# Gated linear attention and a soft mixture of experts on one core: the DRAM rows of q, k, f, v and the weights cut to 512 bytes

## The chip, the core and the metric

The kernel runs on one core of a Trainium2 chip. The metric is device time in microseconds (us), the median over runs of the same program; lower is better. A profile is one execution, recorded instruction by instruction and DMA packet by DMA packet. The engines are PE (matrix multiplies, with PEld for their weight loads), DVE, ACT and POOL (elementwise work) and SP, which here only issues DMAs; SPq is its queue in the profile. Sixteen DMA engines move what SP issues.

## The reference

Two parts follow each other. The first is a recurrence over 768 positions for 4 batches of 8 heads, each with a 48x48 state. The second takes its output as 3072 tokens of 384 numbers, mixes all tokens into 32 slots, runs a two-layer network of 8 experts over the slots, and mixes the slots back into tokens.

```python
f = 1.0 / (1.0 + np.exp(-f_logit))
for t in range(S):                                   # S = 768, D = 48
    state = f[:, :, t, :, None] * state + np.einsum('bhd,bhe->bhde', k[:, :, t], v[:, :, t])
    y[:, :, t] = np.einsum('bhd,bhde->bhe', q[:, :, t], state)
...
logits = x @ phi                                     # x: y as [3072, 384]; phi: [384, 32]
d = softmax over tokens;  slot_input = d.T @ x       # [32, 384]
h = np.maximum(slot_input[e] @ w1[e], 0.0)           # 8 experts, w1[e]: [384, 1024]
slot_out[e] = h @ w2[e]                              # w2[e]: [1024, 384]
out = softmax over slots @ slot_out                  # [3072, 384]
```

All data is float32. The time is taken without the host's rearrangement of the inputs (`_layout`), which only decides in what order numbers lie in DRAM.

## The kernel before

**Blocks.** The recurrence is cut into 24 blocks (NN = 24): 4 batches of 6 blocks of 128 positions, each block for all 8 heads at once. A block needs four inputs: f (the gate's logits), k, q (each 128 partitions x 512 numbers, 256 KB) and v (128 x 384, 192 KB). ACT turns f into logarithms of gates (lines 472 and 475), DVE scans them (464, 465), ACT takes exponentials of the scan (478, 479), POOL or DVE multiplies k and q by those (502, 505), PE transposes k (510), forms scores (524), the update of the state (536) and the outputs (555, 564, 574). Groups of four blocks then feed the softmax over tokens (623 to 657).

**Loads and buffers.** f is loaded one block at a time for the first two blocks and by pairs of blocks after that, into three buffers of two blocks each; k, q and v have four buffers each, used in turn. Tiles have short names: af and ag hold f, ak k, aq q, av v, ac the scans, as the scores, hm the "homes" that hold weights. In DRAM a block of k, q or f is one contiguous stretch of 256 KB with a row of 2 KB for every partition, and a block of v one of 192 KB with rows of 1536 bytes.

**Weights.** w1 and w2 are 12 pieces of 1 MB each. A piece is stored as [4, 128, 512]: four groups of 128 rows of 2 KB, and partition p gets row p of each group. The 12 pieces of w1 go into 12 homes while the recurrence runs (line 422), each held back until a given block has been planned. Three pieces of w2 go into three more homes, seven go into the buffers that the recurrence leaves free (af, ac, ag, ak, aq, as, av), and the last two into homes that w1 leaves free (line 426).

**What follows the recurrence.** PE multiplies the slots by w1 ("up", line 771), the result is transposed and masked, multiplied by w2 ("down", line 805), and the slots are mixed back into tokens (828) and stored in 12 DMAs of 384 KB (837).

**What sets the order.** Operations are added to a planner (`Plan.schedule`) with engines, dependencies, an estimated duration and a priority; it places each on an engine's queue, and the kernel then emits instructions in that order. Every engine works its queue in order. All loads and stores go through SP's single queue, so a load that waits for a buffer holds back all loads behind it, and SP's DMA number i also waits until its DMA number i - 8 has landed (the eight semaphores DMAHW0 to DMAHW7). For a load the planner uses its bytes, not its rows.

Of the kernel before, what the change touches and what calls it, by code (L numbers as in the profile page):

```python
# [15 lines left out]
B, H, S, D = 4, 8, 768, 48  # L16
BT = 128
HT = 64
NB = S // BT
NN = B * NB  # L20
DP = 64
PR = H // 2
# [9 lines left out]
CUT = (0, 128, 256, 384)  # L32
NPART = len(CUT) - 1
HOME = 2048
NHOME = 15
NX = 4

# [14 lines left out]
def flat(t):  # L52
    n = len(t.shape)
    if n == 2:
        return t
    names = "abcde"[: n - 1]
    return t.rearrange(f"p {' '.join(names)} -> p ({' '.join(names)})")
# [207 lines left out]
def gla_soft_moe_kernel(ctx: ExitStack, tc: tile.TileContext, q, k, f, v, fd, qd, kd, vd, phi, w1, w2, out):  # L265
# [9 lines left out]
    nc = tc.nc  # L275
# [18 lines left out]

    AF_, AC, AG, AK, AQ, AS, AV = (P([128, HOME], n) for n in ("af", "ac", "ag", "ak", "aq", "as", "av"))
    homes = [P([128, HOME], f"hm{i}") for i in range(NHOME)]
    NF, NK, NQ, NV, NSS, NXT = 3, 4, 4, 4, 3, 6
# [8 lines left out]
    fb = [group(AF_, 0), group(AF_, 1), group(AG, 0)]  # L306
    cb = [group(AC, i) for i in range(2)]
    kb = [part(AK, 512 * i, 512, a=PR) for i in range(NK)]
    qb = [part(AQ, 512 * i, 512, a=PR) for i in range(NQ)]
    vb = [part(AV, 384 * i, 384, a=H) for i in range(NV)]  # L310
# [103 lines left out]
    W1 = [(j, hf, c) for j in range(2) for hf in range(2) for c in range(3)]  # L414
    W2 = [(p, j, kh) for p in range(NPART) for j in range(2) for kh in range(2)]

    def runs(t):
        return t.rearrange("p (q n) -> p q n", q=4)

    def load_w1(x):  # L420
        t = w1p[W1[x]]
        return lambda e: nc.sync.dma_start(runs(t), w1[x].rearrange("q p n -> p q n"))

    def load_w2(p, j, kh):
        t = w2p[p, j, kh]
        return lambda e: nc.sync.dma_start(runs(t), w2[W2.index((p, j, kh))].rearrange("q p n -> p q n"))


    def T(n, stage):
        return 3.8 * n + stage  # L430

    def load(dst, src, name, key, prio, nbytes):
        add(name, {"SP": 0.42}, lambda e: nc.sync.dma_start(dst, src), w=key, prio=prio, bytes=nbytes)  # L433
# [3 lines left out]

    def load_f(n, cnt):
        i, o = n // 2 % NF, n % 2
        load(fb[i][:, o : o + cnt], f[n : n + cnt].rearrange("n p a t -> p n a t"), f"f{n}", [("f", i, x) for x in range(o, o + cnt)], T(n, -12), 262144 * cnt)  # L440

    def loads(n):
        load(kb[n % NK], k[n], f"k{n}", [("k", n % NK)], T(n, -9), 262144)
        load(qb[n % NQ], q[n], f"q{n}", [("q", n % NQ)], T(n, -8.5), 262144)
        load(vb[n % NV], v[n], f"v{n}", [("v", n % NV)], T(n, -7), 196608)

    def last_of(c_):

# [405 lines left out]
    for n in range(NN):  # L854
        cnt = 1 if n < 2 else 2 - n % 2 * 2
# [6 lines left out]
        x = len(plan.ops)  # L862
# [24 lines left out]
    ending = len(plan.ops)  # L887
    early = NHOME - len(W1)
    for x in range(early):
        w2p[W2[x]] = homes[len(W1) + x]  # L890
        add(f"w2{W2[x]}", {"SP": 0.42}, load_w2(*W2[x]), w=[("home", len(W1) + x), ("w2", W2[x])], prio=1.1e3 + x, bytes=128 * HOME * 4, after=[paced[22]])
    for x, key in enumerate(W1):
        add(f"w1{x}", {"SP": 0.42}, load_w1(x), w=[("home", x)], prio=1e3 + x, bytes=128 * HOME * 4, after=[paced[7 * x // 4]])
    t0, down, put_o, sums, put_s, combine, put_f, store = tail()
# [102 lines left out]
def _layout(inputs):  # L997
    import numpy as np

    a = {}  # L1000

    def rows(x, pad, later):

        x = x.reshape(B, 2, 2, 2, NB, BT, D).transpose(2, 0, 4, 3, 6, 1, 5)
        x = np.stack([x[0], later(x[1])], 4)
        x = np.concatenate([x, np.full((B, NB, 2, DP - D, 2, 2, BT), pad, np.float32)], 3)
        return x.reshape(NN, 128, PR, BT)

    a["q"] = rows(inputs["q"], 0, lambda x: x[..., ::-1])
    a["k"] = rows(inputs["k"], 0, lambda x: x[..., ::-1])  # L1010
    a["f"] = rows(inputs["f_logit"], 30, lambda x: x[..., ::-1, :])
    x = inputs["v"].reshape(B, PR, 2, NB, BT, D).transpose(1, 0, 3, 4, 2, 5)
    x = np.stack([x[p][:, :, ::-1] if p % 2 else x[p] for p in range(PR)], 3)
    a["v"] = x.reshape(NN, BT, H, D)
    for n, name in (("fd", "f_logit"), ("qd", "q"), ("kd", "k"), ("vd", "v")):
        a[n] = inputs[name].reshape(B * PR, 2, S, D).transpose(0, 1, 3, 2)

    heads = [2 * (2 * m + (o ^ r)) + r for r in range(2) for m in range(2) for o in range(2)]
    order = np.concatenate([np.arange(D * h, D * h + D) for h in heads])
    x = inputs["moe_phi"][order].reshape(PR, 2, D, NS)  # L1020
    x = np.concatenate([x, np.zeros((PR, 2, DP - D, NS), np.float32)], 2)
    a["phi"] = x.reshape(PR, 128, NS).transpose(1, 0, 2)
    x = inputs["moe_w1"][:, order].reshape(4, 2, 3, 128, 2, 512)
    a["w1"] = x.transpose(1, 4, 2, 0, 3, 5).reshape(12, 4, 128, 512)
    x = inputs["moe_w2"].reshape(4, 2, 2, 4, 128, NPART, 128)
    a["w2"] = x.transpose(5, 1, 2, 0, 4, 3, 6).reshape(12, 4, 128, 512)
    return {n: np.ascontiguousarray(x) for n, x in a.items()}


# [22 lines left out]
```

## Time and profile before

| what | value |
|---|---|
| median of 3 runs | 188.34 us (187.5 to 189.64) |
| the profiled execution's own time | 188.79 us |
| its span, first to last instruction | 187.1 us |
| granted TensorE clock, mean | 0.957 of full speed |
| PE, PEld, DVE, ACT, POOL busy | 78%, 59%, 63%, 53%, 26% of the span |
| DMA packets; bytes | 28234; 54.12 MB |
| DMA engines busy with SP's packets | 81.2% of 16 engines' span |

The profiled execution took 0.45 us more than the median, and 1.7 us more than its span; the latter is what lies outside the first and last instruction. Times inside the trace count from the span's start.

A DMA is carried out as packets. Each run of contiguous bytes of the DRAM side is one packet here: of SP's 28192 packets, 21504 are rows of 2 KB (128 for each of 24 blocks of q, k and f, and 512 for each of 24 weight pieces), 3072 are v's rows of 1536 bytes, 1536 are output rows of 3 KB, 128 are phi's rows of 512 bytes, and 1952 are the 4-byte semaphore updates with which each of the 16 DMA engines reports the end of its share of each of the 122 DMAs.

"DMA share" in a view by stretches of time is the sum of packets' times divided by 16 engines' time. It can exceed 1, because neighbouring packets of an engine overlap a little. "To landing" is the time from the start of a DMA's issue on SP to the last of its 16 semaphore updates.

The stages are: start-up, about the first 20 us; the recurrence, to about 141 us; "up", 142.2 to 152.7 us; "down", 155.6 to 166.3 us; mixing back and stores, to the end.

### The profile page before, as it was taken

The page shows a single profiled execution, that of the slowest core. Times are in us where ns is not written, and L with a number is a line of the kernel's source. Part 1 is how long each engine was busy: PE and PEld are TensorE (multiplying, and loading weights), DVE is VectorE, ACT ScalarE, POOL GpSimd, SP SyncE. Part 2 cuts the span into 40 slices and gives each one's busy share as a digit, 9 for nine tenths or more (in the row PEclk, how much of TensorE's full clock was granted, in tenths as well). Part 3 has the DMA queues.
Part 4 walks back from the last instruction along what each step waited for, and adds up shares of the span by engine and source line. Part 5 has one row for each costly group of instructions (what it writes and reads, how often), then busy time and mean ns, then how long its engine had stood idle before and what let it go on. Part 6 is the DMA issues. An engine that isn't in the chain of part 4 may idle for free.

```text
span 187.1 us, 7446 instructions
## 1 busy us (share of the span) xinstructions
PE 146.7 (78%) x3238; PEld 109.8 (59%) x3238; DVE 117.3 (63%) x223; ACT 99.1 (53%) x187; POOL 48.0 (26%) x56
## 2 busy tenths in 40 slices
PE   4976886999869978794975996969778999999500
PEld 4864765768758766574854684756533338974100
DVE  6679956999778888974959879474163114026400
ACT  5889855796865948684874464423531120016600
POOL 4142091334460271434056911520011000000000
PEclk9999999999987999999999699999999999999955
DMA  5999999799976999996896779996999248006990
GB/s 186 321 392 383 387 381 383 237 340 398 368 251 172 336 391 312 381 385 203 229 399 208 255 255 316 398 386 215 328 398 388 99 120 332 4 4 267 395 354 16
DMA packets 28234, 54.12 MB, mean 289 GB/s; under 512 B 1952, under 2 KB 5152, under 8 KB 28192
## 3 DMA queue, kind: packets, MB, share of 16 engines
q1 hardware_dynamic: 28192, 53.55, 81.2%
q8 instruction: 27, 0.44, 0.9%
q14 instruction: 15, 0.12, 0.2%
HBM read 48.82 MB, written 4.72 MB: 286 GB/s over the span
## 4 chain that ended last, share of the span: by engine, by line
PE 54%; issue 14%; DVE 10%; DMA 7%; ACT 4%; SPq 3%; POOL 1%; DVEq 0%; POOLq 0%; ACTq 0%
PE pr L524 7%; PE sg L805 6%; PE sg L771 6%; PE pr L574 6%; PE pr L555 5%; PE sg L510 4%; PE pr L564 4%; DMA ak<-in_k_dram 3%; DMA af<-in_f_dram 3%; PE sg L606 3%; PE pr L828 3%; PE sg L536 3%; PE sg L623 3%; SPq L433 3%; PE sg L651 3%
## 5 line engine op out<-in xcount | busy, mean ns | idle before, releaser
L502 POOL TENSOR_TENSOR ak<-ak,af 128x512 f32<-128x512 f32 x14 | 19.0, 1362 | 44.4 <-ACT af L478 35.5
L527 DVE TENSOR_TENSOR as<-pr,tri 128x768 f32<-128x768 f32 x24 | 22.7, 946 | 10.0 <-PE pr L524 9.9
L524 PE MATMUL pr<-aq,ak 48*64 48x64 f32 (+1 forms) x768 | 23.2, 252 | 5.5 <-issue 4.9
L524 PEld LDWEIGHTS pr<-aq,ak 48*64 48x64 f32 x768 | 20.0, 137 | 7.6 <-issue 6.2
L510 PE MATMUL sg<-ident,ak 128*128 128x128 f32 x96 | 15.8, 283 | 4.8 <-issue 2.8
L577 ACT COPY xT<-pr 128x512 f32<-128x512 f32 x22 | 12.7, 585 | 12.6 <-PE pr L574 12.6
L513 ACT COPY ag<-sg 128x512 f32<-128x512 f32 x19 | 11.1, 584 | 11.9 <-PE sg L510 11.8
L555 PE MATMUL pr<-aq,st 48*48 48x128 f32 x320 | 14.1, 278 | 3.5 <-issue 3.4
L505 POOL TENSOR_TENSOR aq<-aq,ac 128x512 f32<-128x512 f32 x11 | 15.0, 1369 | 6.5 <-DMA aq<-in_q_dram 4.7
L574 PE MATMUL pr<-as,av 128*48 128x64 f32 x384 | 15.6, 226 | 0.5 <-issue 0.5
L564 PE MATMUL pr<-as,av 64*48 64x64 f32 x384 | 11.6, 233 | 4.8 <-issue 2.4
L510 PEld LDWEIGHTS sg<-ident,ak 128*128 128x128 f32 x96 | 10.3, 140 | 8.2 <-issue 5.2
L606 PE MATMUL sg<-ident,xT 128*128 128x128 f32 x96 | 14.7, 280 | 0.0
L502 POOL TENSOR_TENSOR ak<-ak,ag 128x512 f32<-128x512 f32 x8 | 10.8, 1362 | 14.7 <-ACT ag L478 6.3
L574 PEld LDWEIGHTS pr<-as,av 128*48 128x48 f32 x384 | 12.5, 126 | 2.3 <-issue 1.7
L465 DVE TENSOR_TENSOR_SCAN ac<-chain,af 128x256 f32<-128x256 f32 x16 | 13.7, 858 | 0.0
L479 ACT ACTIVATE ac<-ac 128x1024 f32<-128x1024 f32 (+1 forms) x13 | 12.9, 994 | 0.3
L464 DVE TENSOR_TENSOR_SCAN ac<-chain,af 128x256 f32<-128x256 f32 x16 | 11.5, 717 | 2.4 <-ACT af L475 2.3
L564 PEld LDWEIGHTS pr<-as,av 64*48 64x48 f32 x384 | 8.5, 127 | 7.5 <-DVE as L527 3.9
L555 PEld LDWEIGHTS pr<-aq,st 48*48 48x48 f32 x320 | 8.6, 119 | 6.3 <-issue 5.6
L505 DVE TENSOR_TENSOR aq<-aq,ac 128x512 f32<-128x512 f32 x13 | 11.9, 937 | 0.1
L536 PE MATMUL sg<-av,ag 128*48 128x48 f32 x320 | 11.4, 215 | 0.5 <-ACT ag L513 0.5
(130 smaller groups left out, 256.1 us busy)
## 6 DMA issues: line engine op xcount, KB each, us to landing
hm<-in_w_dram SPq DMA_DIRECT2D x17, 1024.0 KB, 8.7
ak<-in_k_dram SPq DMA_DIRECT2D x24, 256.0 KB, 6.0
aq<-in_q_dram SPq DMA_DIRECT2D x24, 256.0 KB, 5.7
av<-in_v_dram SPq DMA_DIRECT2D x24, 192.0 KB, 5.9
out_dram<-hm SPq DMA_DIRECT2D x12, 384.0 KB, 4.1
af<-in_f_dram SPq DMA_DIRECT2D x7, 512.0 KB, 6.5
ag<-in_f_dram SPq DMA_DIRECT2D x4, 512.0 KB, 6.3
af<-in_w_dram SPq DMA_DIRECT2D x1, 1024.0 KB, 7.7
```

What stands on the lines that cost most here:

```text
L465: nc.vector.tensor_tensor_scan(cx[:, 2 * BT :][:, ::-1], chain, lx[:, 2 * BT :], 0.0, op0=ALU.mult, op1=ALU.add)
L479: add(f"p{n}", {"ACT": t_act(w)}, lambda e: nc.scalar.activation(flat(c_), flat(c_), AF.Exp, scale=-1.0), w=cs, prio=T(n, 1.2))
L502: tt(e)(flat(k_), flat(k_), flat(g_), op=ALU.mult)
L505: tt(e)(flat(q_), flat(q_), flat(c_), op=ALU.mult)
L510: nc.tensor.transpose(pk[:, a], k_[:, a], ident)
L524: nc.tensor.matmul(o, k_[rows[r], col(a), at], x, start=True, stop=True)
L527: tt(e)(sc_.rearrange("p r m t -> p (r m) t"), bank(("sc", n)).rearrange("p r (m t) -> p (r m) t", m=2)[:, :, :SW], tri.unsqueeze(1).broad ...
L536: nc.tensor.matmul(pk[rows[r], col(a)], kp_[:, col(a), rows[r]], v_[:, 2 * a + r], start=True, stop=True)
L555: nc.tensor.matmul(py[at : at + D, r, a // 2], s0[rows[r], col(a)], queries(r, a), start=a < 2, stop=False, skip_group_check=True)
L564: nc.tensor.matmul(py[at : at + D, r, a // 2, :HT], v_[by, 2 * a + r], sc_[by, r, a // 2, HT:BT], start=first and a < 2, stop=False, skip_ ...
L574: nc.tensor.matmul(py[at : at + D, r, a // 2, HT:], v_[:, 2 * a + r], sc_[:, r, a // 2, x : x + HT], start=False, stop=a >= 2, skip_group_ ...
L606: nc.tensor.transpose(px[:, i], xT[:, n % NXT, i], ident)
```

## The change

The arrays of q, k, f, v, w1 and w2 are laid out in DRAM in rows of 128 numbers, 512 bytes, where they had rows of 512 numbers (384 for v). A block of q, k or f becomes [4, 128, 128]: four groups of 128 rows, and partition p gets row p of each group. v becomes [3, 128, 128] and a weight piece [16, 128, 128]. Neighbouring rows of one partition then lie 64 KB apart. Each load still brings the same numbers to the same places of the same tile, where a partition's numbers lie side by side as before. phi and the stores are left as they are.

The load's access pattern names the rows on both sides, so that a 256 KB load has 512 rows in place of 128, a load of two blocks of f 1024 in place of 256, a load of v 384 in place of 128, and a weight piece 2048 in place of 512.

```diff
+RUN, VRUN = 128, 128
...
-    def runs(t):
-        return t.rearrange("p (q n) -> p q n", q=4)
+    def runs(t, n=RUN):
+        return t.rearrange("p (x n) -> p x n", n=n)

     def load_w1(x):
         t = w1p[W1[x]]
-        return lambda e: nc.sync.dma_start(runs(t), w1[x].rearrange("q p n -> p q n"))
+        return lambda e: nc.sync.dma_start(runs(t), w1[x].rearrange("x p n -> p x n"))

     def load_w2(p, j, kh):
         t = w2p[p, j, kh]
-        return lambda e: nc.sync.dma_start(runs(t), w2[W2.index((p, j, kh))].rearrange("q p n -> p q n"))
+        return lambda e: nc.sync.dma_start(runs(t), w2[W2.index((p, j, kh))].rearrange("x p n -> p x n"))
...
-        load(fb[i][:, o : o + cnt], f[n : n + cnt].rearrange("n p a t -> p n a t"), f"f{n}", [("f", i, x) for x in range(o, o + cnt)], T(n, -12), 262144 * cnt)
+        load(runs(flat(fb[i][:, o : o + cnt])), f[n : n + cnt].rearrange("n x p t -> p (n x) t"), f"f{n}", [("f", i, x) for x in range(o, o + cnt)], T(n, -12), 262144 * cnt)

     def loads(n):
-        load(kb[n % NK], k[n], f"k{n}", [("k", n % NK)], T(n, -9), 262144)
-        load(qb[n % NQ], q[n], f"q{n}", [("q", n % NQ)], T(n, -8.5), 262144)
-        load(vb[n % NV], v[n], f"v{n}", [("v", n % NV)], T(n, -7), 196608)
+        load(runs(flat(kb[n % NK])), k[n].rearrange("x p t -> p x t"), f"k{n}", [("k", n % NK)], T(n, -9), 262144)
+        load(runs(flat(qb[n % NQ])), q[n].rearrange("x p t -> p x t"), f"q{n}", [("q", n % NQ)], T(n, -8.5), 262144)
+        load(runs(flat(vb[n % NV]), VRUN), v[n].rearrange("x p t -> p x t"), f"v{n}", [("v", n % NV)], T(n, -7), 196608)
...
-        return x.reshape(NN, 128, PR, BT)
+        return x.reshape(NN, 128, PR * BT)
+
+    def runs(x, n=RUN):
+
+        return x.reshape(*x.shape[:2], -1, n).swapaxes(1, 2)
...
-    a["w1"] = x.transpose(1, 4, 2, 0, 3, 5).reshape(12, 4, 128, 512)
+    a["w1"] = x.transpose(1, 4, 2, 3, 0, 5).reshape(12, 128, HOME)
...
-    a["w2"] = x.transpose(5, 1, 2, 0, 4, 3, 6).reshape(12, 4, 128, 512)
+    a["w2"] = x.transpose(5, 1, 2, 4, 0, 3, 6).reshape(12, 128, HOME)
+    for n in ("q", "k", "f", "v", "w1", "w2"):
+        a[n] = runs(a[n], VRUN if n == "v" else RUN)
```

The planner sees the same bytes, dependencies and priorities, so on all five engines the instructions stand in the same order as before; only their line numbers and the loads' shapes differ. On SP's queue, around the point where the first weight pieces are loaded, before:

```order
L433 DMA af<-in_f_dram 128x2x512
L422 DMA hm_74<-in_w_dram 128x4x512
L433 DMA aq<-in_q_dram 128x512
L433 DMA ak<-in_k_dram 128x512
L422 DMA hm_75<-in_w_dram 128x4x512
L433 DMA av<-in_v_dram 128x384 x2
```

And in the changed kernel at the same place:

```order
L434 DMA af<-in_f_dram 128x8x128
L423 DMA hm_74<-in_w_dram 128x16x128
L434 DMA aq<-in_q_dram 128x4x128
L434 DMA ak<-in_k_dram 128x4x128
L423 DMA hm_75<-in_w_dram 128x16x128
L434 DMA av<-in_v_dram 128x3x128 x2
```

Nothing has moved: the last number of a shape, the length of a row, goes from 512 (or 384) to 128, and the number of rows for each partition grows to match.

More of the change, by code (lines that the diff above doesn't have):

```diff
@@ L1013, in _layout @@
     x = np.stack([x[p][:, :, ::-1] if p % 2 else x[p] for p in range(PR)], 3)
-    a["v"] = x.reshape(NN, BT, H, D)
+    a["v"] = x.reshape(NN, BT, H * D)
     for n, name in (("fd", "f_logit"), ("qd", "q"), ("kd", "k"), ("vd", "v")):
```

## The prediction

> **What bounds the kernel now.** The page's part on the DMAs comes first, since only loads change, with the waits for loads in the first 31 us (columns: engine, line, what it waited for, total us, times, longest).
>
> ```profile
> DMA packets 28234, 54.12 MB, mean 289 GB/s; under 512 B 1952, under 2 KB 5152, under 8 KB 28192
> q1 hardware_dynamic: 28192, 53.55, 81.2%
> ACT af L472 <- DMA af<-in_f_dram: 4.8, 5, 1.5
> POOL aq L505 <- DMA aq<-in_q_dram: 4.7, 1, 4.7
> POOL ak L502 <- DMA af<-in_f_dram: 1.4, 1, 1.4
> ```
>
> Over the whole kernel the list of waits has the same three for loads, with the same totals: after 31 us no compute engine waits for a load long enough to be listed. The view by stretches of time says how full the DMA engines are (the last three columns: granted clock, DMA share, GB/s).
>
> ```profile
> 2.00:20.00 18.00, 13.91 (x232) 12.22 (x236) 14.51 (x30) 13.72 (x26) 5.00 (x9) 1.00 1.01 359
> 20.00:30.00 10.00, 8.59 (x243) 7.15 (x244) 7.72 (x14) 6.70 (x11) 4.97 (x4) 1.00 1.05 384
> 30.00:54.00 24.00, 19.90 (x504) 15.17 (x504) 20.63 (x33) 19.03 (x37) 8.89 (x7) 1.00 0.97 337
> 54.00:62.00 8.00, 7.76 (x173) 6.66 (x176) 5.83 (x13) 3.98 (x8) 1.47 (x1) 0.79 0.65 188
> 62.00:86.00 24.00, 19.14 (x463) 14.37 (x460) 19.90 (x36) 18.36 (x33) 10.33 (x8) 1.00 1.03 363
> 98.00:114.00 16.00, 13.73 (x322) 10.82 (x318) 14.19 (x26) 8.76 (x18) 8.33 (x7) 0.89 0.74 244
> 2.00:118.00 116.00, 95.16 (x2253) 76.64 (x2257) 93.58 (x167) 79.76 (x145) 43.20 (x46) 0.97 0.93 321
> ```
>
> A full queue shows 1.04 or so, because packets overlap. So the queue is full to 30 us, has small gaps to 54 us, and real gaps at 54 to 62 and 98 to 114 us. Over 2 to 118 us it is busy 0.93 / 1.04 x 116 = 103.7 us and idle 12.3 us. The gaps come from SP, which holds loads until compute frees a buffer (its own waits in the whole kernel):
>
> ```profile
> SPq L433 <- PE pr L524: 25.0, 11, 4.8
> SPq L433 <- PE pr L574: 8.6, 9, 2.4
> SPq L433 <- PE sg L536: 7.8, 5, 2.7
> ```
>
> The start is bound by loads; from 31 to 141 us PE, ACT, DVE and their handovers set the pace, with loads a few us ahead. The chain that ended last says the same: its only large DMA pieces are these (start, us, what).
>
> ```profile
> 6.79 6.45 DMA ak<-in_k_dram
> 13.30 6.40 DMA af<-in_f_dram
> 21.20 1.06 ACT af L475
> 142.18 10.55 PE sg L771 x96
> 155.57 10.76 PE sg L805 x384
> ```
>
> **The price of a row.** Three stretches with a full queue hold nearly one kind of row each: 2 KB weights (120 to 126 us), 3 KB outputs (172 to 177 us), and phi's 512 byte rows between 2 KB rows (11.9 to 12.7 us). Each pair of lines is all packets of the stretch, and SP's with their share.
>
> ```profile
> DMA packets 1163, 2.33 MB, mean 388 GB/s; under 512 B 33, under 2 KB 33, under 8 KB 1162
> q1 hardware_dynamic: 1162, 2.31, 103.9%
> DMA packets 720, 1.97 MB, mean 395 GB/s; under 512 B 79, under 2 KB 79, under 8 KB 719
> q1 hardware_dynamic: 719, 1.97, 100.9%
> DMA packets 266, 0.31 MB, mean 382 GB/s; under 512 B 32, under 2 KB 147, under 8 KB 266
> q1 hardware_dynamic: 266, 0.31, 108.4%
> ```
>
> By pace, with semaphore updates counted into the rows: 6 us x 16 engines / (1162 - 33) rows = 85 ns for 2 KB; 5 x 16 / (719 - 79) = 125 ns for 3 KB. The line through them has 40 ns for 1 KB and 5 ns for every row, so it gives 25 ns for 512 bytes and 65 ns for 1536. The third stretch has 147 - 32 = 115 rows of 512 bytes and 119 of 2 KB: 0.8 x 16 - 119 x 0.085 = 2.7 us, 23.4 ns each. Without dividing the overlap away, its share gives 1.084 x 12.8 = 13.9 us; less 119 x 0.085 (2 KB rows) and some 0.3 us for 32 updates, 3.5 us, 30 ns each. That counts overlapping time twice; half way between, 27 ns, is my upper end. I take 25 ns, from two rows of a thousand and of 640 packets, with 23.4 and 27 as ends.
>
> So four rows cost 100 ns where one of 2 KB cost 85 (+17.6%), three cost 75 where one of v cost 65 (+15.4%). A load of 256 KB, 8 rows for each engine before, goes from 0.68 to 0.80 us, a pair of f from 1.36 to 1.60, v from 0.52 to 0.60, a weight piece from 2.72 to 3.20.
>
> The Trainium skill's page "DMA: Bandwidth & Descriptors", section "Why small descriptors are slow (HBM only)", has a fixed overhead of about 3 cycles for a packet beside one for each 32 bytes. By it, as an estimate, four rows of 512 bytes take 4 x 19 cycles against 67, +13%. The trace's line has the same form with a larger constant, and goes before it; by the Trainium skill's figure every queue term below would be three quarters as large.
>
> **The sum, part by part.** *SP's issue.* It keeps order and number; what an issue costs with more rows is seen from the issues of 128 rows (v) and 512 rows (w2), min, median and max in ns:
>
> ```profile
> L433 SPq DMA_DIRECT2D av<-in_v_dram x24: 327/328/1350, 2.2 to 112.5; - x24
> L426 SPq DMA_DIRECT2D as<-in_w_dram x1: 367/367/367, 132.9 to 132.9; - x1
> ```
>
> 40 ns for 384 rows more; 2048 rows would add some 0.2 us, while a piece keeps the engines busy 3.2 us. Nothing.
>
> *Start-up.* The queue is full from 2 us until f for blocks 6 and 7, issued at 13.30, lands at 19.70 us (the chain above). ACT waits for it, and the chain runs through it.
>
> ```profile
> 19.79 1.06 ACT L472 ACTIVATE af<-af 128x1024 f32<-128x1024 f32 x1 [0.77 <-DMA af<-in_f_dram]
> 29.33 1.06 ACT L472 ACTIVATE af<-af 128x1024 f32<-128x1024 f32 x1 [1.05 <-DMA af<-in_f_dram]
> 33.57 0.59 ACT L513 COPY ag<-sg 128x512 f32<-128x512 f32 x1 [1.99 <-PE sg L510]
> 39.70 1.06 ACT L472 ACTIVATE ag<-ag 128x1024 f32<-128x1024 f32 x1
> ```
>
> 17.7 us x 17.4% = +3.1 us on the end. The next pair of f (29.33) comes 27.3 x 17.4% = 4.7 us later, but ACT idles 1.99 us before the copy at 33.57, which is itself 3.1 us late by then, so 5.1 us cover it. Start-up: +3.1 us (1.8 at 23.4 ns, which is +10%; 4.8 at 27 ns, +27%).
>
> *The recurrence.* The last load of k, issued at 109.31, lands 6.4 us later at 115.7; the multiply for it is in the POOL pair that starts at 117.14, at 118.4 us. That is a lead of 2.7 us. The pair of f that ACT takes at 39.70 was issued at 33.05 and lands at 37.95, a lead of 1.75 us.
>
> ```profile
> 109.31 0.33 SPq L433 DMA_DIRECT2D ak<-in_k_dram  x1
> ak<-in_k_dram SPq DMA_DIRECT2D x1, 256.0 KB, 6.4
> 117.14 2.50 POOL L502 TENSOR_TENSOR ak<-ak,ag 128x512 f32<-128x512 f32 x2 [0.47 <-ACT ag L478]
> 33.05 1.57 SPq L433 DMA_DIRECT2D ag<-in_f_dram  x1
> ag<-in_f_dram SPq DMA_DIRECT2D x1, 512.0 KB, 4.9
> ```
>
> Up to the last load of v there are 72 block loads of q, k and f, 24 of v and 12 weight pieces: before 72 x 0.68 + 24 x 0.52 + 12 x 2.72 = 94.1 us at full pace, against 103.7 busy; 9.6 us are packets slower than the pace, which I keep. After: 57.6 + 14.4 + 38.4 = 110.4, with them 120.0 us, where 116 + 3.1 are there. The queue becomes about as long as the recurrence, and its 12.3 us of gaps shrink but cannot vanish, since SP still waits for buffers. With none, k's last load lands 120 - 116 = 4 us later, less the lead of 2.7: 1.3, inside the start-up's 3.1. With half of the gaps left, 6.2 us, it is 7.5 us. I take the middle between 3.1 and 7.5, since the gaps sit where compute holds the buffers, and that stays so: 5.3 us, of which 2.2 come on top of start-up. That share of the gaps is a choice; no row shows it.
>
> *Late weights.* Ten pieces of w2 are issued from 112.98 on, 4.8 us more in all. The queue stands still between 148 and 152 us, and the last two pieces, issued at 151 to 152 into homes, land 7.1 us later at most, at 159.0; homes are multiplied from 160.83 on.
>
> ```profile
> 148.00:152.00 4.00, 4.00 (x40) 1.17 (x36) 0.00 (x0) 0.81 (x2) 0.00 (x0) 1.00 0.00 0
> hm<-in_w_dram SPq DMA_DIRECT2D x1, 1024.0 KB, 7.1
> 160.83 3.68 PE L805 MATMUL sg<-hm,xT 128*32 128x128 f32 x128
> ```
>
> The pause takes most of the 4.8 us, and 159.0 + 1.0 us is still before 160.8: nothing. Without that cover each late piece would cost 0.48 us. Stores keep their rows: nothing.
>
> Sum: 3.1 + 2.2 = +5.3 us on the profiled execution's 188.8, 194.1. That execution lies 0.45 us above the median of 188.34; on the median it is 193.6, and I say **193.8 us**.
>
> At 23.4 ns the loads need 94.1 x 1.10 + 9.6 = 113 us, less than is there: only 1.8 us, 190.1. At 27 ns they need 94.1 x 1.265 + 9.6 = 128.6 us; 12.6 later, less 2.7 of lead, with up to 4 us of gaps: +9.9 to +13.9, 198 to 202. The likeliest case's own range is 190 to 202 us.
>
> **Rivals.** *Rows of 512 bytes run at line rate, nothing changes.* The third stretch above moved 382 GB/s with half of its rows at 512 bytes, beside 388 for 2 KB alone. For it speaks that number; against it that 2 KB rows still carry 0.24 of the 0.31 MB there, so that a price of 25 ns in place of 21 would show as 115 x 4 = 0.5 us in 12.8. Then the time stays, 187.5 to 189.5. The Trainium skill, page "DMA: Bandwidth & Descriptors", section "Specifications", has 512 bytes as the smallest transfer at line rate; by that rule this is the case, and the line through the trace's 2 KB and 3 KB rows does not agree with it. The decision falls at 21 to 22 ns a row. Chance 0.16.
>
> *Faster.* The place is the packets slower than the pace: 9.6 us up to 118 us, and 359 GB/s up to 20 us against 388 later. If short rows, spread over the DRAM in another way, ended those and cost no more than 21 ns, start-up would shrink by (1 - 359 / 388) x 17.7 = 1.3 us, and later loads are hidden anyway: 187.0. With any price above 23 ns the gain is gone. No row shows such a gain. Chance 0.06.
>
> *The rows cannot be fed.* At 25 ns, 16 engines take 640 rows a microsecond. The densest stretch in this trace is the third, 234 rows in 0.8 us, 293 a microsecond, in which nothing was short. Until the last v the loads have 72 x 512 + 24 x 384 + 12 x 2048 = 70,656 rows. At 500 a microsecond that is 141 us, 25 later than now, less 2.7: 211. The line decides against it down to about 560 a microsecond. The issue rows (40 ns for 384 rows) speak against it, but say only what SP spends. Chance 0.10.
>
> **How the numbers follow.** The forecast has 0.68, line rate 0.16, faster 0.06, starved 0.10. A measurement of this kernel can tell about 1% from no change, 1.9 us: faster is under 186.5, same up to 190.2. The forecast's low end touches 190, so I leave 0.02 of it in "same". Faster 0.06 (at 187.0 it lies at the border, and I count it whole), same 0.16 + 0.02 = 0.18, slower 0.66 + 0.10 = 0.76. The range runs from 188 to 205: the forecast's own, the larger part of line rate, and 3 us above 202 for more gaps. Outside are "faster", a quarter of line rate and nearly all of "starved": 0.06 + 0.04 + 0.09 = 0.19.
>
> **What would show it.** SP's packets become 28192 + 3 x 21504 + 2 x 3072 = 98,848. GB/s in 2 to 20 us falls from 359 to about 305 and in 20 to 30 us from 384 to about 327; f for blocks 6 and 7 lands near 22.8 us. DMA share in 54 to 62 and 98 to 114 us rises towards 1. Waits for DMA, 10.9 us in all before, grow, and some lie after 31 us. "Up" starts near 147.5 us and lasts its 10.5 us, "down" too. Wrong would be: a full queue at 385 GB/s (line rate); a full queue below 290 GB/s with engines idle between packets (starved); late weights in the chain of waits.

## The result, and the profile after

The changed kernel took 199.36 us (median of 4 runs, 197.98 to 203.36) beside 188.99 us for the kernel before in the same runs (median of 4, 187.5 to 193.56). The ratio is 1.055, with a 95% interval of 1.043 to 1.068. A second measurement, made beside the later experiments, gave 201.29 against 188.95 us, ratio 1.073 (1.056 to 1.091). Medians and ranges here are of all executions, but ratios and intervals leave out those that took over 1.5% longer than the same kernel's fastest. The profiled execution took 199.9 us, 11.1 more than the profiled one before. So the change is slower by 10 to 12 us by the medians, about twice the 5.5 that were forecast. That is inside the range, and at the upper end of the likeliest case's own range: close to the 198 to 202 that the prediction gave for rows of 27 ns. The last part says how much of that closeness is luck.

The page's lines on the span, the DMAs and the chain that ended last, of the changed kernel:

```profile
span 198.1 us, 7470 instructions
GB/s 153 294 291 275 226 298 244 309 291 291 291 276 292 293 294 281 293 293 291 249 301 294 280 270 296 284 294 295 294 289 294 291 293 291 294 67 114 384 382 94
DMA packets 62026, 54.12 MB, mean 273 GB/s; under 512 B 1952, under 2 KB 48160, under 8 KB 61984
q1 hardware_dynamic: 61984, 53.55, 97.9%
PE 38%; DMA 24%; SPq 9%; ACT 9%; issue 6%; DVE 5%; POOL 5%; POOLq 0%; DVEq 0%; ACTq 0%
```

Its list of the engines' waits for block loads (as in the prediction: total us, times, longest):

```profile
ACT af L473 <- DMA af<-in_f_dram: 17.4, 8, 5.0
POOL ak L503 <- DMA ak<-in_k_dram: 6.3, 3, 5.1
ACT ag L473 <- DMA ag<-in_f_dram: 5.4, 3, 2.2
DVE aq L506 <- DMA aq<-in_q_dram: 3.3, 4, 1.1
PE sg L537 <- DMA av<-in_v_dram: 2.2, 2, 2.0
```

The second line of the page has the rate in slices of 5 us. From 5 us until 175 us they stand near 290 GB/s whatever the stage, at the lowest 226. Only the stores at the end, whose rows are as before, run at 384. The engines wait 34.6 us for these loads (17.4 + 6.3 + 5.4 + 3.3 + 2.2) where it was 10.9, and loads are 24% of the chain, where before its only large ones were two in the first 20 us.

Stretches of time (columns as in the prediction: busy times, then granted clock, DMA share, GB/s):

```profile
2.00:20.00 18.00, 15.42 (x214) 13.79 (x216) 11.99 (x24) 11.56 (x22) 3.71 (x8) 0.81 1.08 280
20.00:30.00 10.00, 7.21 (x185) 5.85 (x180) 7.08 (x15) 7.69 (x13) 3.01 (x3) 1.00 0.96 264
54.00:62.00 8.00, 6.02 (x157) 5.01 (x161) 6.24 (x11) 6.17 (x15) 2.89 (x2) 1.00 1.04 283
98.00:114.00 16.00, 12.51 (x317) 9.92 (x307) 13.02 (x24) 11.14 (x24) 6.33 (x5) 1.00 1.06 284
148.00:160.00 12.00, 11.13 (x95) 3.69 (x98) 2.83 (x11) 1.79 (x5) 0.61 (x1) 0.72 1.06 292
2.00:118.00 116.00, 95.53 (x2112) 77.92 (x2113) 87.78 (x158) 76.43 (x141) 37.47 (x34) 0.91 1.07 283
```

The gaps of before (share 0.65 at 54 to 62 us, 0.74 at 98 to 114, 0.00 at 148 to 152) are gone. Smaller ones are left: the slices of 226 and 244 GB/s lie at 20 to 25 and 30 to 35 us, and 2 to 118 us has 283 GB/s where 290 would be full. So the queue is close to full from 2 to 175.7 us, and mostly simply takes that long. SP's own view from 128 us on shows the same from the issuing side:

```profile
129.86 10.11 SPq L427 DMA_DIRECT2D hm<-in_w_dram  x3
140.41 3.11 SPq L427 DMA_DIRECT2D ac<-in_w_dram  x1
158.44 3.12 SPq L427 DMA_DIRECT2D av<-in_w_dram  x1
162.02 6.72 SPq L427 DMA_DIRECT2D hm<-in_w_dram  x2
```

Single issues start some 3.6 us apart, as long as a piece of 2048 rows keeps 16 engines busy at the price measured below (2048 x 28.2 ns / 16), and each holds SP for some 3 us. An earlier piece was issued in 0.93 us (at 24.95 us), so it is not the rows that take SP that long; it looks held back by the full queue.

The long pieces of its chain that are loads (start, us, what):

```profile
16.95 7.15 DMA af<-in_f_dram
25.97 8.25 DMA av<-in_v_dram
42.67 6.15 DMA ag<-in_f_dram
69.63 9.18 DMA ag<-in_f_dram
91.88 6.37 DMA ak<-in_k_dram
162.02 10.42 DMA hm<-in_w_dram
```

On the timelines of ACT, POOL and PE, the users of the loads on which the prediction's terms rest, and "up":

```profile
24.18 1.06 ACT L473 ACTIVATE af<-af 128x1024 f32<-128x1024 f32 x1 [2.11 <-DMA af<-in_f_dram]
131.09 1.27 POOL L503 TENSOR_TENSOR ak<-ak,ag 128x512 f32<-128x512 f32 x1 [4.22 <-PE sg L511]
150.71 12.89 PE L772 MATMUL sg<-hm,si 128*32 128x512 f32 x96
172.49 3.82 PE L806 MATMUL sg<-hm,xT 128*32 128x128 f32 x127 [0.56 <-DMA hm<-in_w_dram]
```

f for blocks 6 and 7 is used at 24.18 us, where it was 19.79. The last k is multiplied at 131.09, right after it lands at 130.95 (the profile names a matrix multiply as the releaser, but that was over before; the load came last). "Up" starts at 150.71 instead of 142.18 and lasts 12.89 instead of 10.51 us.

Where the time goes, in two executions of each kernel. The landings are the last of a DMA's semaphore updates; "changed, again" belongs to the second measurement, and "before, again" is the last experiment below:

| us | before | before, again | changed | changed, again |
|---|---|---|---|---|
| f for blocks 6 and 7 lands | 19.70 | 19.62 | 24.09 | 23.39 |
| last k lands | 115.7 | 114.9 | 131.0 | 131.0 |
| last v lands | 118.0 | 118.3 | 133.2 | 132.9 |
| "up" starts | 142.2 | 144.8 | 150.7 | 151.5 |
| "up" lasts | 10.5 | 12.7 | 12.9 | 12.9 |
| from the end of "up" to the span's end | 34.4 | 34.7 | 34.5 | 34.7 |
| last weight lands | 159.0 | 164.0 | 175.7 | 176.6 |
| span | 187.1 | 192.2 | 198.1 | 199.1 |
| granted clock, mean | 0.957 | 0.906 | 0.901 | 0.910 |

So the first pair's 11.0 us of span are 8.5 us of a later "up", 2.4 us of a longer one, and 0.1 after it. But the first pair differs in its clock too. The two profiles of the kernel before, one program, lie 5.1 us apart, with the loads in the table's first three rows landing within 1 us of each other: at the lower clock "up" starts 2.6 us later and lasts 2.2 longer. The second pair, with nearly equal clocks, differs by 7.0 us, 6.8 of it a later "up". The clock does not account for the change, though: of the executions on record with a granted clock of 0.928 to 0.942, the 22 of the kernel before took 186.8 to 192.2 us (median 189.0) and the 4 of the changed one 198.0 to 202.4.

### The profile page after: what moved, and what is told of

It is laid out like the page before. It is cut to its first block, busy times and chain, and to the rows that moved or that the text cites. A ratio compares the mean times of both kernels' runs of the same rounds, so it can differ in the third digit from the quotient of the medians.

```text
span 198.1 us, 7470 instructions
## 1 busy us (share of the span) xinstructions
PE 156.7 (79%) x3238; PEld 117.3 (59%) x3238; DVE 117.7 (59%) x223; ACT 98.5 (50%) x187; POOL 47.0 (24%) x56
## 2 busy tenths in 40 slices
DMA packets 62026, 54.12 MB, mean 273 GB/s; under 512 B 1952, under 2 KB 48160, under 8 KB 61984
## 3 DMA queue, kind: packets, MB, share of 16 engines
q1 hardware_dynamic: 61984, 53.55, 97.9%
## 4 chain that ended last, share of the span: by engine, by line
PE 38%; DMA 24%; SPq 9%; ACT 9%; issue 6%; DVE 5%; POOL 5%; POOLq 0%; DVEq 0%; ACTq 0%
SPq L434 8%; DMA ag<-in_f_dram 8%; PE sg L772 6%; DMA hm<-in_w_dram 5%; DMA av<-in_v_dram 4%; DMA af<-in_f_dram 4%; PE sg L511 4%; POOL ak L503 4%; PE pr L525 3%; PE pr L556 3%; PE sg L607 3%; DMA ak<-in_k_dram 3%; PE pr L829 3%; PE sg L806 3%; PE pr L575 3%
## 5 line engine op out<-in xcount | busy, mean ns | idle before, releaser
L511 PE MATMUL sg<-ident,ak 128*128 128x128 f32 x96 | 17.4, 308 | 9.3 <-POOL ak L503 6.9
L525 PEld LDWEIGHTS pr<-aq,ak 48*64 48x64 f32 x768 | 21.6, 147 | 4.9 <-issue 2.5
L511 PEld LDWEIGHTS sg<-ident,ak 128*128 128x128 f32 x96 | 11.6, 154 | 13.1 <-POOL ak L503 8.2
L473 ACT ACTIVATE af<-af 128x1024 f32<-128x1024 f32 (+1 forms) x9 | 8.7, 963 | 19.3 <-DMA af<-in_f_dram 17.4
L578 ACT COPY xT<-pr 128x512 f32<-128x512 f32 x22 | 12.7, 587 | 9.8 <-PE pr L575 9.7
L506 POOL TENSOR_TENSOR aq<-aq,ac 128x512 f32<-128x512 f32 x11 | 14.1, 1290 | 10.9 <-ACT af L479 6.2
L575 PE MATMUL pr<-as,av 128*48 128x64 f32 x384 | 16.7, 237 | 0.0
L556 PE MATMUL pr<-aq,st 48*48 48x128 f32 x320 | 15.2, 301 | 1.5 <-ACT xT L578 0.7
L514 ACT COPY ag<-sg 128x512 f32<-128x512 f32 x19 | 11.0, 581 | 10.5 <-PE sg L511 10.5
L537 PE MATMUL sg<-av,ag 128*48 128x48 f32 x320 | 11.7, 218 | 5.4 <-ACT ag L514 2.4
L465 DVE TENSOR_TENSOR_SCAN ac<-chain,af 128x256 f32<-128x256 f32 x16 | 11.3, 707 | 6.5 <-ACT af L476 4.7
L537 PEld LDWEIGHTS sg<-av,ag 128*48 128x48 f32 x320 | 9.5, 131 | 8.9 <-issue 3.9
L575 PEld LDWEIGHTS pr<-as,av 128*48 128x48 f32 x384 | 13.6, 135 | 2.0 <-issue 1.0
L565 PE MATMUL pr<-as,av 64*48 64x64 f32 x384 | 11.7, 239 | 2.2 <-DVE as L528 1.4
L480 ACT ACTIVATE ac<-ac 128x1024 f32<-128x1024 f32 (+1 forms) x13 | 12.9, 995 | 0.3
L506 DVE TENSOR_TENSOR aq<-aq,ac 128x512 f32<-128x512 f32 x13 | 11.1, 863 | 3.3 <-DMA aq<-in_q_dram 3.3
L607 PEld LDWEIGHTS sg<-ident,xT 128*128 128x128 f32 x96 | 11.2, 147 | 2.9 <-ACT ag L514 1.2
```

Of the source, the lines that this page charges most:

```text
L480: add(f"p{n}", {"ACT": t_act(w)}, lambda e: nc.scalar.activation(flat(c_), flat(c_), AF.Exp, scale=-1.0), w=cs, prio=T(n, 1.2))
L506: tt(e)(flat(q_), flat(q_), flat(c_), op=ALU.mult)
L511: nc.tensor.transpose(pk[:, a], k_[:, a], ident)
L525: nc.tensor.matmul(o, k_[rows[r], col(a), at], x, start=True, stop=True)
L537: nc.tensor.matmul(pk[rows[r], col(a)], kp_[:, col(a), rows[r]], v_[:, 2 * a + r], start=True, stop=True)
L556: nc.tensor.matmul(py[at : at + D, r, a // 2], s0[rows[r], col(a)], queries(r, a), start=a < 2, stop=False, skip_group_check=True)
```

## Experiments

### What a row costs

The prediction's price of a row was a line through two points. The first experiment measures rows of six lengths, each in a queue with nothing else in it. The loop of a stage, for rows of 512 bytes and then for one with two issuing queues:

```diff
+    def rows_512():
+        for i in range(NH):
+            nc.sync.dma_start(cut(homes[i], 128), w128[i].rearrange("x p n -> p x n"))
+    def rows_512_two_queues():
+        for i in range(NH):
+            (nc.scalar if i % 2 else nc.sync).dma_start(cut(homes[i], 128), w128[i].rearrange("x p n -> p x n"))
```

> The kernel holds nothing but loads of weights, eight of 1 MB a phase (0.75 MB for 384-byte rows), in nine phases: rows of 2 KB; 512 bytes; 512 bytes issued in turn from SP and ACT; 512 bytes in four loads of 256 KB; 512 bytes with a partition's rows 640 bytes apart instead of 64 KB; 1 KB; 8 KB; 384 bytes; 256 bytes. It computes nothing of the reference and stores some of the weights as its output. Theory 'engine': a row costs a DMA engine a fixed time beside its bytes, as 85 ns for 2 KB and 27.6 ns for 512 bytes in the changed kernel say: 46.7 ns for 1 KB, 22.5 for 384 bytes, 17.9 for 256 bytes, whoever issues them. Theory 'feed': rows reach the 16 engines at 580 a microsecond at most, one each 27.6 ns for an engine: 512, 384 and 256 bytes all at 27.6 ns a row, 1 KB at 45 ns; with two issuing queues 512 bytes at 25 ns or less if each queue has its own feed. Theory 'distance': the 64 KB from row to row cost the 2.6 ns above the line through 2 KB and 3 KB: rows 640 bytes apart 25 ns, 256 bytes about 15 ns plus the same extra.

Stretches in the middle of each stage (columns without PE: us, busy DVE, ACT, POOL, clock, DMA share, GB/s). In order: rows of 2 KB; 512 bytes; 512 bytes from two queues; 512 bytes in loads of 256 KB; 512 bytes with neighbouring rows 640 bytes apart; 1 KB; 8 KB; 384 bytes; 256 bytes.

```profile
6.00:18.00 12.00, 0.77 (x5) 0.00 (x0) 0.00 (x0) 1.00 1.03 387
32.00:52.00 20.00, 0.68 (x5) 0.05 (x2) 0.00 (x0) 1.00 1.06 290
56.00:72.00 16.00, 0.74 (x6) 0.05 (x2) 0.00 (x0) 1.00 1.06 290
80.00:106.00 26.00, 1.23 (x8) 0.00 (x0) 0.00 (x0) 1.00 1.19 290
112.00:130.00 18.00, 0.61 (x4) 0.00 (x0) 0.00 (x0) 1.00 1.19 290
140.00:152.00 12.00, 0.61 (x4) 0.00 (x0) 0.00 (x0) 1.00 1.10 347
168.00:176.00 8.00, 0.61 (x4) 0.00 (x0) 0.00 (x0) 1.00 1.02 424
190.00:200.00 10.00, 0.70 (x5) 0.00 (x0) 0.00 (x0) 1.00 1.16 321
212.00:230.00 18.00, 0.61 (x4) 0.00 (x0) 0.00 (x0) 1.00 1.11 218
```

Four ways of asking for 512 byte rows all give 290 GB/s: a second issuing queue, four times as many loads and rows that lie close together change nothing. Rows of 256 bytes come at 851 a microsecond (218 GB/s), where rows of 512 bytes come at 566, so no limit on rows a microsecond holds the latter back. So it is not the feeding and not the distance, but the DMA engines' time for a row: 16 x 512 / 290 = 28.2 ns. The others by the same division: 84.7 ns for 2 KB, 47.2 for 1 KB, 309 for 8 KB, 18.8 for 256 bytes. All five lie on 9.4 ns for a row and 9.4 ns for each 256 bytes in it (18.8, 28.2, 47.0, 84.6, 310). The rows of 384 bytes do not: 19.1 ns, close to a row of 256 bytes. Why was not tried.

The 290 GB/s are the changed kernel's plateau, so the row's price carries over into the kernel.

### Blocks alone, weights alone

The changed kernel with the weights back at 2 KB, and with the blocks back:

```diff
-RUN, VRUN = 128, 128
+RUN, VRUN, W1RUN, W2RUN = 128, 128, 512, 512
```
```diff
-RUN, VRUN = 128, 128
+RUN, VRUN, W1RUN, W2RUN = 512, 384, 128, 128
```

> Only q, k, f and v in rows of 512 bytes, the weights in rows of 2 KB as before. Theory 'the queue as a whole': at 27.6 ns a row start-up is 5 us later (30% of 17.7 us), and the loads up to the last v need 63.7 + 15.8 + 32.6 + 9.6 = 121.7 us, which start-up's delay and a part of the gaps take in: +5 to +7, 194 to 196 us. Theory 'each row adds its cost': blocks have 18 of the 28 us that all loads grow by, so 65% of the whole slowdown: +6.8 us, 195.5. The two come apart in the next kernel.

> Only the weights in rows of 512 bytes, q, k, f and v as before. Theory 'the queue as a whole': start-up is untouched, the loads up to the last v need 49 + 12.5 + 42.5 + 9.6 = 113.6 us of 116, so the gaps take nearly all of it: 0 to +2 us, 188 to 191; this and the blocks alone together are less than the whole change. Theory 'each row adds its cost': 35% of the slowdown, +3.7 us, 192.5, and the two add up to the whole.

Measured: blocks alone 195.8 us (193.03 to 198.13), ratio 1.041 (1.017 to 1.064); weights alone 191.81 us (189.68 to 194.97), ratio 1.020 (1.000 to 1.040), beside 188.0. Added, that is 6.1%, and both together gave 5.5 and 7.3%, so nothing speaks against a plain sum. For the weights alone the two theories said up to 191 and 192.5 us, and the interval has room for both. With the blocks alone "up" starts at 148.4 us and the tail after it is that of before (34.5 us). With the weights alone "up" starts at 143.3, the last k and v land as before (115.9 and 117.8 us), but "up" lasts 12.0 us, with a spell at half clock, and "down" 12.4 instead of 10.7. That is not shown to be a wait for weights: the last one lands at 163.5, and the one long pause in "down" ends later, with no releaser that the profile names:

```profile
165.31 3.36 PE L806 MATMUL sg<-hm,xT 128*32 128x128 f32 x114 [1.29 <-issue]
```

So the blocks hurt ahead of "up"; which wait makes up the 2% of the weights alone is not traced.

### The late weights alone put back

The changed kernel with w2 in rows of 2 KB:

```diff
-RUN, VRUN = 128, 128
+RUN, VRUN, W1RUN, W2RUN = 128, 128, 128, 512
```

> The changed kernel with w2 alone back in rows of 2 KB (its pieces are all issued after the last v). Theory 'late weights': in the changed kernel the queue stays full to 175 us and the product with w2 waits for its last pieces; with 2 KB rows ten pieces need 27 us in place of 35, the wait goes, 198 us or 1.2 us below the changed kernel. Theory 'nothing': the last pieces were not what held it, same as the changed kernel, 199.4 us.

Measured: 198.04 us (197.03 to 198.39), ratio 1.060 (1.046 to 1.075). The last weight lands at 169.0 instead of 175.7 us, and the wait for it in "down" is gone:

```profile
170.41 3.76 PE L806 MATMUL sg<-hm,xT 128*32 128x128 f32 x128
```

Almost nothing is gained: 1.3 us by the medians, 3.3 against the second measurement, and the intervals separate neither from zero. "Down" lasts 11.3 us, still longer than the 10.7 of before. The last k still lands at 130.4 us and "up" starts at 149.1: w2 is queued behind all block loads, so its rows cannot bring those forward.

### The start alone, short and long

First the kernel before with only the first eight blocks' q, k, f and v in short rows, then the changed kernel with only these in long ones (the loads, not shown, ask `short(n)` for block n):

```diff
+RUN, VRUN, W1RUN, W2RUN = 128, 128, 512, 512
+START = 8
+def short(n):
+    return n < START
```
```diff
+RUN, VRUN, W1RUN, W2RUN = 128, 128, 128, 128
+START = 8
+def short(n):
+    return n >= START
```

> Only q, k, f and v of the first 8 of 24 blocks in rows of 512 bytes, all else as before. Theory 'start-up passes on': f for blocks 6 and 7 lands 4.4 us later (24.1 for 19.7 us, as in the changed kernel) and the recurrence, bound by compute from there on, ends as much later: +3 to +4.5 us on before. Theory 'the gaps take it': the recurrence catches up, 0 to +1 us.

> The changed kernel with q, k, f and v of the first 8 blocks back in rows of 2 KB and 1.5 KB. Theory 'the queue is full all along': the loads up to the last v need 6.5 us less in all, and the time falls by 4 to 6 us, to 194 or 195, still 6 us above before. Theory 'start-up alone': with the start as before the rest is hidden again, 188 to 190.

Start short: 192.09 us (189.32 to 196.12), ratio 1.013 (1.002 to 1.025), so 2.5 us on 189. The interval is 0.4 to 4.7 us, which has room for both theories. f for blocks 6 and 7 lands at 23.7 us, 4.0 later, and in this profile "up" starts at 146.5, 4.3 later, though its last k lands only 2.9 later (118.6); its granted clock of 0.908 has a part in that. So by the middle of the interval more than half of that lateness passes to the end, as the prediction had it for start-up.

Start long: 194.51 us (191.24 to 195.75) beside 189.12, from four executions, too few and too far apart for an interval. It is what "the queue is full all along" said. f for blocks 6 and 7 lands at 19.36 as before. This profile (193.69 us) is the one that shows two things at once:

```profile
123.94 1.26 POOL L517 TENSOR_TENSOR ak<-ak,ag 128x512 f32<-128x512 f32 x1 [4.45 <-DMA ak<-in_k_dram]
141.74 10.51 PE L786 MATMUL sg<-hm,si 128*32 128x512 f32 x96
158.68 1.08 PE L820 MATMUL sg<-as,xT 128*32 128x128 f32 x32 [2.48 <-DMA as<-in_w_dram]
165.71 3.79 PE L820 MATMUL sg<-hm,xT 128*32 128x128 f32 x126 [0.79 <-DMA hm<-in_w_dram]
```

The last k lands at 123.8 us, 8.1 later than before, and "up" starts at 141.7, not later at all. So in the kernel before, the last k has some 8 us of cover, not the 2.7 us of lead that the prediction read at its multiply. With the blocks alone the last k landed no later than here (122.0 us) and "up" started 6.2 us late all the same; there the start was late, with f for blocks 6 and 7 at 23.0 us, and here it is not. The two profiles have like clocks (0.932 and 0.926). So lateness reached "up" there by another way than the last k; the late start, handed on from engine to engine, is the likely one. The second: with "up" as early as before, "down" now runs into weights that are not there: it waits 3.3 us for them (2.48 and 0.79). It lasts 16.7 us instead of 10.7, of which some 1.7 us fall to a spell of 3.4 us at half clock. The queue lets go of its last weight at 169.0 us, 13.9 us after "down" has begun, where it was 3.5.

### Both at once

The changed kernel with the start and w2 in long rows; and, beside it on the same chip, the changed kernel once more:

```diff
-RUN, VRUN = 128, 128
+RUN, VRUN, W1RUN, W2RUN = 128, 128, 128, 512
+START = 8
+def short(n):
+    return n >= START
```

> The changed kernel with two parts put back to long rows: the q, k, f and v of the first eight blocks (2 KB and 1.5 KB rows) and the w2 pieces (2 KB rows); w1, phi and the loads of the later blocks stay at 512 B. 'Two paths' (the time of the changed kernel is held by two chains that end nearly together: the late start through the recurrence, and the full queue through the last weights; either alone undone leaves the other): both are relieved at once, the first blocks' f lands near 19.4 us, the loops over 96 weights start near 141.7 us as they did with the long start alone, their stretch of 10.5 us follows, the last weight lands near 162 to 164 us instead of 169, and the time is 189 to 191. 'Every row adds' (each part put back is worth its own difference and no more: 5 us for the start and 1.4 us for the late weights, of 199.4): 193.

> The changed kernel itself once more, beside the partial ones on the same chip. The first measurement gave 1.055 of the kernel before with an interval of 1.043 to 1.068; if it stands, 198 to 200 against 188 to 189. In the first profile the loops over 96 weights took 12.9 us instead of 10.5, in a stretch where the clock fell to half for a while. 'The clock's dip belongs to the change': the stretch takes 12.5 us or more again. 'The dip falls where it falls': 10.5 to 12 us, and a time 1 to 2 us shorter in that execution.

Measured: 190.39 us (188.21 to 192.39) beside 188.95, ratio 1.018 (1.005 to 1.031), against 201.29 us (198.93 to 202.76) for the changed kernel. The last weight lands at 163.4 us and "down" lasts its 10.7; "up" starts at 143.6 rather than 141.7. Apart the two steps had given 1.3 us and about 5 us (194.51 beside 199.36, in different measurements); together they give 10.9 us on one chip. That is what "two paths" expects and what a plain sum, 6.3 us, does not. But the medians come from three measurements: against 201.29 the two steps apart are 3.3 and 6.8 us, and a plain sum, 10.0, fits as well. What shows the second path is the profiles: with the start alone long, "down" waits 3.3 us for weights, and with w2 long as well it does not wait. The rest, w1 and two thirds of the blocks in short rows, costs 1.8%.

### Rows of 1 KB, and rows of 8 KB

The changed kernel with rows of 1 KB (768 bytes for v); then the kernel before with longer rows: weights at 8 KB and pairs of f at 4 KB, and after that the weights alone.

```diff
-RUN, VRUN = 128, 128
+RUN, VRUN, W1RUN, W2RUN = 256, 192, 256, 256
```
```diff
+RUN, VRUN, W1RUN, W2RUN = 512, 384, 2048, 2048
...
-        load(fb[i][:, o : o + cnt], f[n : n + cnt].rearrange("n p a t -> p n a t"), f"f{n}", [("f", i, x) for x in range(o, o + cnt)], T(n, -12), 262144 * cnt)
+        load(flat(fb[i][:, o : o + cnt]), f[n // 2, :, 512 * o : 512 * o + 512 * cnt], f"f{n}", [("f", i, x) for x in range(o, o + cnt)], T(n, -12), 262144 * cnt)
```

> Rows of 1 KB for q, k, f and the weights, of 768 bytes for v. By 'engine', 9.4 ns a row and 9.4 ns for each 256 bytes (the loads alone: 28.2 ns for 512 bytes, 47.0 for 1 KB, 84.5 for 2 KB), a 256 KB load takes 0.75 us in place of 0.68, a weight piece 3.0 in place of 2.7: start-up +11% of 17.7 us = 1.9 us, loads up to the last v 104.7 + 7 to 9.6 us, less than the 116 that are there: +2 to +3.5 us on before, a third of the whole change. Theory 'feed' (rows a microsecond) would have 1 KB rows free: 0.

> The other way: the weights in rows of 8 KB, pairs of f in rows of 4 KB, the rest as before. By 'engine' a weight piece takes 2.49 us in place of 2.70, a pair of f 1.28 in place of 1.35; start-up is 0.3 us shorter and the rest of the loads are hidden in the kernel before: 0 to -0.7 us, not to be told from before. If every us of load time counted (2.6 us less up to the last v): -2 to -3 us.

> The kernel before with the weights alone in rows of 8 KB; f, q, k, v as before. The longer rows everywhere gave 0.991. 'The weights' (the queue after 88 us is what sets the last loads of v and the weights, so shorter weight loads give the gain): the last v lands near 115.5 us instead of 118, ratio 0.991 to 0.994. 'The start' (the gain came from the f pairs in the first 20 us, which lie ahead of everything): 1.000, with the last v early all the same.

1 KB: 194.87 us (191.01 to 199.44) beside 189.12; the executions spread too far for an interval, so no more can be said than that its median lies between the two kernels, 5.8 us above the kernel before, where 2 to 3.5 were expected. f for blocks 6 and 7 lands at 21.0 us.

Longer rows: 186.62 us (12 runs, 184.8 to 188.35), ratio 0.991 (0.985 to 0.996). Weights alone: 185.67 us (12 runs, 183.23 to 190.68), ratio 0.990 (0.981 to 0.998). Both beat both kernels, by about 1%, some 2 us, where 0 to 0.7 was expected from the price of a row with the loads hidden. The gain comes from the weights: without the longer rows of f it is all there. The last v lands at 115.1 and 114.7 us, where it was 118.0. "Up" starts at 138.3 us with both longer; with the weights alone:

```profile
138.54 11.70 PE L772 MATMUL sg<-hm,si 128*32 128x512 f32 x96
```

That is 3.6 us earlier than before. It is more than the last loads' 3 us, so single executions differ by some of it.

### The kernel before, once more

> The kernel before once more, with a second profile of its own. In its first profile the loops over 96 weights took 10.5 us without a spell at half clock in them; in the changed kernel's two profiles they took 12.9 us both times. 'The clock's dip belongs to the change' (more idle time on PE ahead of them): 10.5 us again, or 11.9 at most. 'The dip falls where it falls' (a spell at half clock comes somewhere near 140 to 160 us in most executions of either kernel): about 12 to 13 us, and then the 2.4 us are not to be counted as a cost of the rows. The time is 188 to 189 and the ratio 1.00 with an interval that shows how finely this kernel can be told from itself.

Measured: 189.96 us (186.8 to 193.9) beside 190.42, ratio 0.995 (0.977 to 1.012). Its profiled execution was the slowest of its six (193.9 us), and its "up" lasts 12.69 us. The stretch of time around its first 4 us (the last three columns: clock, DMA share, GB/s):

```profile
144.00:148.00 4.00, 4.00 (x42) 1.49 (x37) 0.58 (x3) 0.00 (x0) 0.29 (x1) 0.50 0.69 259
```

The same of the changed kernel:

```profile
150.00:154.00 4.00, 4.00 (x37) 1.42 (x33) 0.58 (x3) 0.00 (x0) 0.22 (x1) 0.50 1.06 292
```

Both run at half clock there, so the spell does not need the short rows. In the changed kernel's two profiles it was there both times, in the kernel before once in two. "Up" lasted 10.5 us in the kernel before, with the longer rows and with the long start, 11.7 to 12.2 in four others and 12.7 to 13.2 in six. So these 2.4 us of the first pair's 11 cannot be counted as a cost of the rows. Nor is this spell the clock's only effect: the same profile starts "up" 2.6 us later than the first one with the same rows, after more time at half clock during the recurrence. The mean granted clock was 0.935 over the 59 executions of the kernel before on record and 0.917 over the 10 of the changed one; whether the change lowers it stays open.

## Why the prediction was right or wrong

**What bounds the kernel.** Right in the main: the start by loads, the recurrence by compute. "Loads a few us ahead" was too little: at the end it was some 8 us. And not all loads were hidden, since weights in rows of 8 KB made the kernel 1% faster; which wait that took away was not followed.

**The price of a row, 25 ns with ends of 23.4 and 27: wrong, 28.2.** This is the step that failed first. The slope came from the 3 KB stores at 172 to 177 us, taken as a full queue. Their share was 100.9% where the 2 KB stretch had 103.9%, in the very lines quoted, and by the law measured since a 3 KB row costs 9.4 + 12 x 9.4 = 122 ns, not 125 (the law is of loads and these are stores; the packets themselves took 121 ns at the median). That raised the slope from 37.6 to 40 ns for 1 KB and took away half of each row's fixed cost: 5 ns instead of 9.4. The third stretch had the true price between its two readings, 23.4 ns with the overlap divided away and 30 without; going half way between gave an upper end below it. So four rows cost 113 ns where one of 2 KB cost 85, +33% instead of +17.6%.

The Trainium skill's page "DMA: Bandwidth & Descriptors", section "Why small descriptors are slow (HBM only)", has about 3 cycles for a packet, by the prediction's estimate +13% here. The first experiment has a fixed cost as large as that of 256 bytes, where the Trainium skill's 3 cycles equal 96 bytes. The form agrees, the size does not, and the measurement decides. The Trainium skill's "Specifications" on the same page, 512 bytes as the smallest transfer at line rate, does not hold in these runs: 290 GB/s at 512 bytes, 347 at 1 KB, 387 at 2 KB and 424 at 8 KB.

**Start-up, +3.1 us: right in kind, 4.4 and 3.7 measured,** by the two landings of f for blocks 6 and 7. At 28.2 ns the step's own working would give 17.7 x 33% = 5.8; before, the queue ran at 359 GB/s there and not at 388, and short rows lost less against that. The start alone cost 2.5 us at the end (0.4 to 4.7).

**The recurrence, +2.2 us more: the mechanism held, two terms were wrong and pulled against each other.** "Half of the gaps left" was said to be a choice; almost none was left (DMA shares 1.04 and 1.06 at 54 to 62 and 98 to 114 us; 1.07 and 0.92 in the second profile). SP's waits for buffers did not keep the gaps open: by its list of waits they shrank from 62 to 38 us at the block loads, and those that stayed seldom emptied the queue. With the right price the loads up to the last v take 64.9 + 16.2 + 43.3 = 124.4 us, and with the 9.6 us of slower packets 134, which is 18 more than the 116 of before; measured were 15.2 (last v 133.2 instead of 118.0). On the other side the lead of the last k was taken as 2.7 us, from its landing to its multiply. That is the multiply's own slack, but the work behind it had more: from the last k's landing to "up" it took 26.5 us before, and 17.9 to 20.5 in the five runs whose last k lands after 123 us. So 6 to 8 us of late loads cost nothing there. 15.3 us late (131.0 against 115.7), less 6.7 us made up (26.5 - 19.8), is the 8.5 us by which "up" starts late. This is a sum and not yet a cause: with the blocks alone "up" was 6.2 us late with a last k inside its cover, and the clocks of the two profiles differ, so how the 8.5 us divide between late start, late k and clock stays open. The price alone, put right and with no gaps left, would have given 134 - 116 - 2.7 = 15.3 in place of 5.3, some 203.6 us. So that the result lies in the 198 to 202 given for 27 ns is luck in part: the price was still too low there, and the lead too short.

**Late weights, "nothing": wrong in its reason, nearly right in its number.** The pause at 148 to 152 us that was to take them is filled to a share of 1.05 and more, and the last weight lands at 175.7, not 160. They cost only 0.6 us of waiting in "down", which the rest gives back (34.5 us after "up", as before), because "up" itself was late. With the start put back "down" waits 3.3 us for them, so the cover named for the term was the wrong one. "Late weights in the chain of waits" was named as a sign that the prediction would be wrong, and they are in it (162.02).

**SP's issue, "nothing": right,** though late issues took 3 us instead of 0.4. The queue was hardly ever idle, and two queues gave the same 290 GB/s.

**Stores, "nothing": right.** 384 GB/s and the same tail.

**"Up" and "down" last as before: wrong by 2.4 and 1.2 us.** The first is the half clock, which the kernel before also shows; of the second 0.6 us are the wait for the last weights, and the rest is not explained (with w2 in long rows "down" lasts 11.3 us without any wait for a load).

**Rivals.** Line rate fell: 290 GB/s. Faster fell: no row gets cheaper. "Cannot be fed" had its sign, a full queue at 290 or a little below, but the engines were not idle between packets (share 1.06), a second queue fed no more, and rows of 256 bytes came faster.

**The packets.** 98,848 were forecast for SP, 61,984 recorded: 46,208 of 512 bytes for q, k, f, v and phi, but the weights' 49,152 rows as 12,288 records of 2 KB, each four rows long in time (median 116 ns where a true row of 2 KB took 84).

## What to carry to other kernels

Read a price per row only from a stretch whose DMA share shows a full queue, and hold two sizes against a third before drawing a line. A load's slack is not its distance to its first use: it is what the whole chain behind that use can still make up. Where two chains end nearly together, undoing one can uncover the other, as the long start uncovered the late weights; undo both in one run before calling either of them harmless. And take a second profile of the kernel before: here two of one program lay 5.1 us apart.

## What the runs showed of the hardware that was not expected

Loaded from DRAM, a row cost a DMA engine 9.4 ns and then 9.4 ns for each 256 bytes, at the five lengths of 256 and 512 bytes, 1, 2 and 8 KB. At 512 bytes one issuing queue or two, and a next row 640 bytes or 64 KB away, made no difference. Rows of 384 bytes break this: they moved 321 GB/s, more than rows of 512 bytes; no run says why.

Even 2 KB rows leave something: 8 KB rows moved 424 against 387 GB/s, and for the weights alone that was worth 1% of this kernel (ratio 0.990, 0.981 to 0.998).

The profile can record four rows as one packet, so its count of packets does not always give the rows. A packet that takes longer than its length should is the sign.
